# Attention, output projection and gated MLP on one core: when a unit's loads and the chain of its outputs are issued

## Chip, core and metric

The kernel runs on one core of a Trainium2 chip. The metric is the device time of one execution in microseconds (us), lower is better. Before the change the median of 3 runs is 2955.37 us (2953.96 to 2956.3).

## The reference, cut

```python
def _A_ref(x, wqkv, wo):                       # B = 1, S = 2048, D = 576
    H = 32; Dh = D // H                        # 32 heads of 18
    qkv = (x @ wqkv).reshape(B, S, 3, H, Dh).transpose(2, 0, 3, 1, 4)
    q, k, v = qkv[0], qkv[1], qkv[2]
    p = _softmax(einsum("bhqd,bhkd->bhqk", q, k) * Dh ** -0.5, axis=-1)
    o = einsum("bhqk,bhkd->bhqd", p, v)
    return o.transpose(0, 2, 1, 3).reshape(B, S, D) @ wo
def _B_ref(x, w_gate, w_up, w_down):           # F = 4608
    return (sigmoid(x @ w_gate) * (x @ w_up)) @ w_down
...
h = _layernorm(x) * (1 + ca) + sa
x = x + ga * _A_ref(h, A_wqkv, A_wo)
h = _layernorm(x) * (1 + cb) + sb
return x + gb * _B_ref(h, B_w_gate, B_w_up, B_w_down)
```

All is float32; the six vectors sa, ca, ga, sb, cb, gb come from a small product of a condition vector with `w_mod`.

## The kernel before

The program has three stages: layer norm and projections of q, k and v (to about 229 us of the trace), attention (229 to 1604 us), and the MLP (to the end). The change is in attention.

**Units and steps.** Attention is cut into 32 units, `u` = 0 to 31. A unit is a pair of heads on one half (1024) of the queries: units 0 to 15 take the first half, 16 to 31 the second. A unit has 16 steps (`kt` = 0 to 15 in the code; this text counts them 1 to 16), one for each block of 128 keys. In a step TensorE makes four score tiles (L916) of 128 keys x 512 queries, ScalarE takes their exponentials (L920), and `values()` (L539) multiplies the exponentials of two steps back by the values and by a column of ones, so that the sums of the softmax come out as a row of the output.

**Maxima.** The softmax needs the maximum of each query, and it is made by a second set of score tiles, in `maxima()`: 64 tiles to a unit, four in each step, made 22 steps ahead of the unit that uses them. So the maxima of unit u+1 end in step 10 of unit u, and those of u+2 begin in step 11. VectorE reduces each tile (L452). In most units ("paired" ones) one tile of eight goes to ScalarE instead (L455, a copy through Relu) and is joined to another by VectorE (L457). In units 0, 1, 16 to 18 and 27 to 29 (`SINGLE`) all are reduced alone. After the 64th tile VectorE runs a short chain, here called **the maxima's end**: reduce (L464), transpose (L466), cast (L468), subtract (L469). Then the maxima go through DRAM into rows of the queries' tile (L470, L475).

Score tiles of both kinds rotate through seven banks of PSUM (`bank()`): a tile's matmul waits until the bank's tile of seven tiles ago has been read.

**Loads of heads.** `load_heads(u + 2)` (L413 to L421) issues eight transfers on SyncE's queue (SP), some 1.5 MB, into the tiles that unit u-1 has freed. It stands at the end of step 2.

**Outputs.** The 512 queries x 4 result of unit u-1 is complete in step 1 of unit u. In step 2 ScalarE copies it out (L553), and `outputs()` gives a list of things to do; every even step takes one off the list (the letter `w` in the order of a step). Before the change the list is `[gather, spread, None, None, scaled, None, stored]`, so:

- step 2, `gather`: a transfer (SP, L571) brings the sums into a 128x16 tile;
- step 4, `spread`: VectorE's reciprocal (L574), a transfer of it to DRAM (SP, L575), and a transfer that reads it back over 128 partitions (SP, L576);
- step 10, `scaled`: GpSimd multiplies, casts and subtracts (POOL, L579 to L581);
- step 14, `stored`: four transfers to `od` in DRAM (SP, L592).

**Work beside it.** At the letter `w` also stands one turn of `rows0` (from step `FROM0`, unit 15) or of `rows1` (from step `FROM1`, unit 27). `rows0` first prepares the weights of the output projection on GpSimd (`load_wo`), then idles eight turns, then projects the first half (`project_o(0, 8)`, matmuls L676, loads of `od` L645 and L650 and of x L652 on SP, each tile of 128 rows in two turns and loaded a tile ahead), then runs layer norm and makes operands for the MLP (L767, L716 to L727, GpSimd). `rows1` projects most of the second half (`project_o(8, 16)`).

**What sets the order.** In attention TensorE, VectorE and SP run in the order in which the code is written. ScalarE and GpSimd are put in order by the scheduler when the program is built. Every engine runs its own instructions strictly in its order, and each instruction of SP's waits, with all behind it, for what it needs.

## Time and profile before

| | |
|---|---|
| median of 3 runs | 2955.37 us |
| the profiled execution's own time | 2952.37 us |
| its span in the trace | 2950.6 us |
| busy: TensorE (PE), VectorE (DVE), ScalarE (ACT), GpSimd (POOL) | 97%, 75%, 53%, 23% |
| granted TensorE clock, mean | 0.987 |
| an ordinary paired unit | 39.5 to 40.2 us |
| units 17 and 18, 28 and 29 (with projection) | 53.4 and 54.7, 54.3 and 54.3 us |

A row of a timeline gives start, duration, engine, line, operation, `out<-in`, shapes, how many in a row, and in brackets the idle time of the engine before it with what ended it. A row of a table of windows gives a stretch `from:to`, its length, and for each engine the busy time with the count of instructions, then the granted clock (1.00 is full speed), the busy share of the DMA engines, and GB/s. `SPq` is SyncE's queue, where a row's duration is that of issuing a transfer, not of the transfer itself.

### The profile page before, as it was taken

To read this page: it belongs to the slowest core of one execution; us is meant where nothing else is said; L and a number is where in the kernel's file an instruction comes from. 1 tells how busy PE (TensorE), PEld (TensorE's weight loads), DVE (VectorE), ACT (ScalarE), POOL (GpSimd) and SP (SyncE) were. 2 spreads that over 40 slices of the span, in tenths; PEclk is the share of its full clock that TensorE was granted. 3 is DMA by queue.
4 is the path that set the end of the run, shared out by engine and by line. 5 is a ranking of instruction groups with operands and counts; after the bars stand their busy time and mean duration, and the time that the engine had idled before them with its cause. 6 is when DMAs were issued, how large, how long until landed. Compare 5 with 4: busy or idle time off the path is not lost.

```text
span 2950.6 us, 46231 instructions
## 1 busy us (share of the span) xinstructions
PE 2848.5 (97%) x16901; PEld 1876.0 (64%) x16901; DVE 2215.6 (75%) x4047; ACT 1570.4 (53%) x2908; POOL 684.8 (23%) x793
## 2 busy tenths in 40 slices
PE   7999999999999999999999899988999999999999
PEld 6863333333344534334443788877888888888888
DVE  7278889999999789999872778878877555555555
ACT  3217889999977688898678323333333111111111
POOL 3112025455221007730103322233222100000000
PEclk9999999999999999999999999999999999999999
DMA  5343244444223312321344776677555845545443
GB/s 178 123 160 87 65 125 156 155 144 135 88 79 92 109 54 92 111 74 59 101 132 153 273 239 228 234 256 249 207 200 211 321 159 176 170 167 167 165 157 136
DMA packets 177135, 456.26 MB, mean 155 GB/s; under 512 B 36488, under 2 KB 86412, under 8 KB 164620
## 3 DMA queue, kind: packets, MB, share of 16 engines
q1 hardware_dynamic: 162140, 376.72, 38.8%
q0 software_dynamic: 14768, 76.59, 7.4%
q8 instruction: 133, 2.18, 0.3%
q14 instruction: 94, 0.77, 0.1%
HBM read 285.07 MB, written 167.91 MB: 154 GB/s over the span
## 4 chain that ended last, share of the span: by engine, by line
PE 77%; DVE 11%; DMA 4%; issue 3%; ACT 3%; SPq 1%; POOL 1%; POOLq 0%; DVEq 0%; ACTq 0%
PE o L539 15%; PE d L1055 14%; PE x L1019 12%; PE s L446 10%; PE s L916 10%; PE bg L1019 4%; PE bu L1019 4%; DVE mx L452 4%; PE s L276 4%; PE s L327 2%; ACT p L920 2%; PE s L676 2%; DVE w L1011 1%; DMA xs<-ho 1%; DMA t<-od 1%
## 5 line engine op out<-in xcount | busy, mean ns | idle before, releaser
L452 DVE TENSOR_REDUCE mx<-s 128x1 f32<-128x512 f32 x1664 | 1057.3, 684 | 130.8 <-PE s L446 109.5
L920 ACT ACTIVATE p<-s 128x512 f32<-128x512 f32 x2048 | 1064.3, 611 | 165.6 <-PE s L916 80.8
L446 PE MATMUL s<-k,q 54*128 54x512 f32 x1920 | 610.4, 451 | 14.7 <-ACT p L920 6.3
L916 PE MATMUL s<-q,k 56*128 56x512 f32 x1920 | 559.0, 429 | 11.6 <-DVE mx L452 8.0
L539 PE MATMUL o<-p,vaug 128*32 128x512 f32 x4096 | 560.4, 612 | 0.4 <-ACT p L920 0.4
L1055 PE MATMUL d<-wd,hh 128*128 128x288 f32 x2304 | 475.5, 301 | 27.9 <-DVE Oa L1059 25.7
L446 PEld LDWEIGHTS s<-k,q 54*128 54x128 f32 x1920 | 278.2, 186 | 281.7 <-ACT p L920 225.1
L916 PEld LDWEIGHTS s<-q,k 56*128 56x128 f32 x1920 | 263.5, 187 | 300.1 <-DVE mx L452 216.1
L1055 PEld LDWEIGHTS d<-wd,hh 128*128 128x128 f32 x2304 | 378.4, 191 | 44.0 <-DVE Oa L1059 33.6
L1059 DVE TENSOR_TENSOR Oa<-Oa,d 128x288 f32<-128x288 f32 x576 | 256.0, 452 | 133.3 <-PE d L1055 129.0
L1055 PE MATMUL d<-wd,hl 128*128 128x288 f32 x1152 | 343.8, 298 | 0.0
L1019 PE MATMUL x<-k,w 128*128 128x512 f32 x1008 | 244.3, 393 | 4.2 <-ACT w L1010 4.2
L1055 PEld LDWEIGHTS d<-wd,hl 128*128 128x128 f32 x1152 | 220.1, 191 | 0.0
L1019 PEld LDWEIGHTS x<-k,w 128*128 128x128 f32 x1008 | 188.8, 190 | 43.8 <-ACT w L1010 5.6
L1031 ACT ACTIVATE u<-u 128x512 f32<-128x512 f32 x72 | 45.4, 631 | 320.2 <-DVE u L1207 316.2
L539 PEld LDWEIGHTS o<-p,vaug 128*32 128x32 f32 x4096 | 84.0, 108 | 167.7 <-issue 155.8
L1028 ACT ACTIVATE sg<-x 128x512 f32<-128x512 f32 x36 | 21.6, 599 | 315.7 <-PE x L1019 315.6
L1061 POOL DMA_DIRECT2D out_dram<-Oa x16 | 8.7, 544 | 604.3 <-DVE Oa L1059 604.3
L455 ACT ACTIVATE over<-s 128x512 f32<-128x512 f32 x192 | 114.6, 597 | 37.9 <-PE s L446 32.3
L457 DVE CUSTOM_DVE_ANT_0 over<-s,over 128x512 f32<-128x512 f32 x192 | 129.4, 674 | 0.0
L1019 PE MATMUL x<-big,w 128*128 128x512 f32 x504 | 120.5, 390 | 2.2 <-issue 2.2
L1019 PE MATMUL x<-w,w 128*128 128x512 f32 x504 | 121.2, 390 | 0.0
(211 smaller groups left out, 3555.0 us busy)
## 6 DMA issues: line engine op xcount, KB each, us to landing
ws<-w SPq DMA_DIRECT2D x126, 640.0 KB
w<-ws SPq DMA_DIRECT2D x126, 640.0 KB
wd<-wds SPq DMA_DIRECT2D x36, 1152.0 KB
k<-kd SPq DMA_DIRECT2D x60, 360.0 KB
wds<-w POOLq DMA_DIRECT2D x18, 1152.0 KB, 5.5
k<-kd SPq DMA_DIRECT2D x60, 180.0 KB
w<-in_B_w_down_dram POOLq DMA_DIRECT2D x18, 576.0 KB, 5.1
q<-qd SPq DMA_DIRECT2D x64, 144.0 KB
```

The lines of the kernel that those rows point to most:

```text
L276: nc.tensor.matmul(acc, w, hT[:, t, cols], start=n == 0, stop=n == len(ts_) - 1)
L327: nc.tensor.matmul(acc[:, 0:HALF], hT[:, k, rows], w, start=n == 0, stop=n == len(ts_) - 1,)
L446: nc.tensor.matmul(sp, qs[rows, qt * P : (qt + 1) * P], ks[rows, at * 512 : (at + 1) * 512], start=True, stop=True,)
L452: nc.vector.tensor_reduce(to, sp, axis=AX.X, op=ALU.max)
L455: nc.scalar.activation(over, sp, AF.Relu)
L457: nc.vector.tensor_tensor_reduce(out=over, in0=sp, in1=over, scale=1.0, scalar=LOWEST, op0=ALU.add, op1=ALU.max, accum_out=mx[:, h * n + q ...
L539: nc.tensor.matmul(acc[32 * j : 32 * j + 32, :], vaug[:, kt, (2 * p + h) * VW : (2 * p + h) * VW + 32], probs[2 * c + h], start=kt == 0, s ...
L916: nc.tensor.matmul(sT, ks[rows, kcols], qs[rows, c * 512 : (c + 1) * 512], start=True, stop=True)
L920: state["exp"] = nc.scalar.activation(pr, sT, AF.Exp, scale=SCALE)
L1019: nc.tensor.matmul(acc[v], w[:, v, a, :], X[s][:, b, :], start=first and n == 0, stop=n == 6, skip_group_check=not first,)
L1055: nc.tensor.matmul(acc[:, :HALF], a[:, f, rows], w[:, f, cols], start=n == 0, stop=n == 5)
L1059: nc.vector.tensor_add(Oa[:, t, cols], Oa[:, t, cols], acc[:, :HALF])
```

## The change

`load_heads(u + 2)` moves from the end of step 2 to the start of the unit. `spread` is split: the reciprocal and its transfer to DRAM become `inverted`, the read back remains `spread`, and the list becomes `[gather, None, None, inverted, spread, None, scaled, stored]`, that is steps 2, 8, 10, 14 and 16. Since outputs are stored one turn later, `load_wo` idles nine turns and `FROM1` is two steps later: both projections, and all that follows in `rows0`, move by two steps.

```diff
-FROM0, FROM1 = 15 * 16, 27 * 16 + 13
+FROM0, FROM1 = 15 * 16, 27 * 16 + 15
...
-        def spread():
+        def inverted():
             nc.vector.reciprocal(rec, sums)
             nc.sync.dma_start(rows_r.rearrange("j (q e) -> (j q) e", e=16), rec)
+
+        def spread():
             nc.sync.dma_start(full, rows_r.unsqueeze(1).to_broadcast([4, 32, 512]))
...
-        return [gather, spread, None, None, scaled, None, stored]
+        return [gather, None, None, inverted, spread, None, scaled, stored]
...
         weights.extend((wo_h, wo_l, we))
-        for _ in range(8):
+        for _ in range(9):
             yield
...
         qs, ks = heads(u)
+        if 0 < u < UNITS - 2:
+            load_heads(u + 2)
...
             pending.append((half, p, kt, probs))
-            if 0 < u < UNITS - 2 and kt == 1:
-                load_heads(u + 2)
```

Lines below the split stand two to four further down after it: `spread` is L578, the stores L594, the loads of `od` L647 and L652, of x L654, the scores L920, the exponentials L924.

On SP, at the turn from unit 16 to unit 17, where the first projection starts, there stood these rows (stores of unit 15's outputs, five loads for the first projected tile, the gather, the next tile's first load):

```order
L592 DMA od<-big 18x2x512 x4
L645 DMA t_11968<-od 128x4x128
L650 DMA t_11968<-od 64x128
L645 DMA t_11968<-od 128x4x128
L650 DMA t_11968<-od 64x128
L652 DMA Oa<-in_A_x_dram 128x576
L571 DMA sums<-oT 128x1x16
L645 DMA t_12043<-od 128x4x128
```

and now stand these:

```order
L594 DMA od<-big 18x2x512 x4
L413 DMA q_984<-qd 36x1x1024
L416 DMA q_984<-qd 18x1024
L417 DMA k_2193<-kd 36x1x2560
L421 DMA k_2193<-kd 18x2560
L413 DMA q_984<-qd 36x1x1024
L416 DMA q_984<-qd 18x1024
L417 DMA k_2193<-kd 36x1x2560
L421 DMA k_2193<-kd 18x2560
L571 DMA sums<-oT 128x1x16
L647 DMA t_12045<-od 128x4x128
L652 DMA t_12045<-od 64x128
```

The first tile's loads have moved from ahead of the eight loads of heads to behind them. On SP in unit 28, in the second projection, the piece behind the loads of heads was (reciprocal out, read back, then a projected tile's loads):

```order
L421 DMA k_2190<-kd 18x2560
L575 DMA rows_r<-rec 128x16
L576 DMA big<-rows_r 128x1x512
L645 DMA t_18809<-od 128x3x128 x2
L652 DMA raw_18812<-in_A_x_dram 128x576
```

and is now:

```order
L421 DMA k_2190<-kd 18x2560
L571 DMA sums<-oT 128x1x16
L647 DMA t_18713<-od 128x3x128 x2
L654 DMA raw_18716<-in_A_x_dram 128x576
L647 DMA t_18870<-od 128x3x128 x2
L654 DMA raw_18873<-in_A_x_dram 128x576
L575 DMA rows_r<-rec 128x16
L578 DMA big<-rows_r 128x1x512
```

Two tiles' loads now stand ahead of the reciprocal's transfer and the read back, none between or just behind them. On ScalarE, in step 9 of unit 9 (numbers on the names are kept; `s0` to `s6` are the banks, `over` is the tile that goes through Relu), there stood:

```order
L920 ACTIVATE p2_7691<-s5_7689 128x512
L455 ACTIVATE over_7702<-s0_7700 128x512
L920 ACTIVATE p1_7706<-s1_7704 128x512
L920 ACTIVATE p0_7710<-s2_7708 128x512
L920 ACTIVATE p3_7720<-s5_7718 128x512
```

and now:

```order
L924 ACTIVATE p2_7690<-s5_7688 128x512
L924 ACTIVATE p1_7705<-s1_7703 128x512
L924 ACTIVATE p0_7709<-s2_7707 128x512
L455 ACTIVATE over_7701<-s0_7699 128x512
L924 ACTIVATE p3_7719<-s5_7717 128x512
```

The Relu, which frees bank s0, has moved behind two exponentials. The scheduler does so in step 9 of 21 units: 1 to 14 and 19 to 25, by one place in units 1, 19 and 23 and by two in the others.

## The prediction

> **What bounds the kernel now.** I read the chain of work that ended last, then what SP's queue waited for, then step by step the windows of attention, and timelines at the steps that stand out.

> ```profile
> PE 77%; DVE 11%; DMA 4%; issue 3%; ACT 3%; SPq 1%; POOL 1%; POOLq 0%; DVEq 0%; ACTq 0%
> SPq L576 <- DMA rows_r<-rec: 232.0, 32, 14.5
> ```

> TensorE carries the chain. SP stands 232.0 us in 32 waits (7.3 us each) at the read back (L576) until the reciprocals have landed in DRAM. That is no loss by itself: what counts is what stands behind it in the queue. The next rows are SP's in unit 28, and TensorE's first matmul of the projected tile loaded there.

> ```profile
> 1435.90 0.36 SPq L575 DMA_DIRECT2D rows_r<-rec  x1
> 1442.78 0.60 SPq L576 DMA_DIRECT2D big<-rows_r  x1
> 1443.47 1.02 SPq L645 DMA_DIRECT2D t<-od  x2
> 1450.88 0.58 PE L676 MATMUL s<-w,t 128*128 128x288 f32 x1 [4.35 <-DMA t<-od]
> ```

> The read back held SP until 1442.78, the tile's loads went out behind it, and TensorE then idled 4.35 us for them. The windows show what such places cost; in each the counted instructions are TensorE's score matmuls (L916). The first seven are steps 11 and 12 of units 0, 13, 24, 16, 22, 23, 27; the last four are steps 6 and 8 of unit 28, and of unit 29.

> ```profile
> 260.42:265.53 5.11, 2.77 (x8) 1.36 (x8) 1.00 0.05 10
> 789.76:794.91 5.15, 2.26 (x8) 1.09 (x8) 1.00 0.06 12
> 1285.11:1290.55 5.44, 2.37 (x8) 1.23 (x8) 1.00 0.04 8
> 915.88:923.72 7.84, 3.60 (x8) 1.67 (x8) 0.78 0.04 8
> 1199.79:1206.46 6.67, 2.37 (x8) 1.23 (x8) 1.00 0.32 115
> 1241.95:1250.59 8.64, 2.44 (x8) 1.37 (x8) 0.84 0.17 51
> 1407.36:1415.21 7.85, 3.57 (x8) 1.62 (x8) 0.78 0.03 6
> 1440.03:1443.65 3.62, 1.15 (x5) 0.37 (x3) 1.00 0.15 35
> 1445.89:1456.21 10.32, 1.44 (x5) 0.47 (x3) 0.67 0.61 146
> 1494.90:1498.80 3.90, 1.43 (x5) 0.55 (x3) 1.00 0.23 51
> 1501.04:1510.93 9.89, 1.71 (x5) 0.65 (x3) 0.65 0.61 162
> ```

> Steps 11 and 12 take 5.11 and 5.15 us undisturbed, but 7.84 and 7.85 in units 16 and 27, 6.67 and 8.64 in 22 and 23. Step 8 takes 10.32 us in unit 28 where step 6 takes 3.62. The granted clock is below 1.00 in most of these. The steps around 11 suffer from GpSimd, as unit 16 shows:

> ```profile
> 916.93 1.19 DVE L468 CAST parts<-turned 128x32 fp32r<-128x32 f32 x1
> 918.16 0.65 DVE L469 TENSOR_TENSOR parts<-turned,parts 128x32 fp32r<-128x32 f32 x1
> 916.80 1.28 POOL L579 TENSOR_TENSOR big<-big,oT 128x512 f32<-128x512 f32 x1
> 918.15 0.61 POOL L580 CAST big<-big 128x512 fp32r<-128x512 f32 x1
> ```

> The cast and subtract of the maxima's end, 0.18 and 0.19 us in unit 14 below, last until GpSimd's multiply and cast of the outputs are over. I call that a collision.

> **The change, part by part**, against the profiled execution (2952.37 us, 3.0 under the median shown).

> (a) *The read back no longer stands ahead of a projected tile's loads.* In units 28 and 29 those loads now go out ahead of the reciprocal. Gone: (10.32 - 3.62) + (9.89 - 3.90) = **-12.7 us**. What is late next there is (b).

> (b) *Heads' loads ahead of a projected tile's loads.* How long they fill the queue is seen in unit 14:

> ```profile
> 808.14 0.80 SPq L413 DMA_DIRECT2D q<-qd  x1
> 813.61 0.36 SPq L575 DMA_DIRECT2D rows_r<-rec  x1
> 821.23 0.59 SPq L576 DMA_DIRECT2D Oa<-rows_r  x1
> 1543.70 0.34 SPq L575 DMA_DIRECT2D rows_r<-rec  x1
> 1545.13 0.57 SPq L576 DMA_DIRECT2D big<-rows_r  x1
> ```

> A small transfer issued right behind the loads has landed 821.23 - 808.14 = 13.1 us after the first of them went out; in unit 30, without such loads (last two rows), it takes 1.43 us. [...] Now unit 17, before:

> ```profile
> 933.85 0.50 PE L916 MATMUL s<-q,k 56*128 56x512 f32 x1
> 936.65 1.85 PE L676 MATMUL s<-w,t 128*128 128x288 f32 x12
> ```

> A projection's matmuls begin 2.80 us into the unit in step 2. After the change the first tile's are in step 4, two steps (5.11 us) later, at 7.9 us. Its loads stand behind the loads of heads, which cannot begin before the unit does. They land not before 13.1 us; by themselves they take up to 7.4 us (1443.47 to 1450.88, with the read back ahead). I take 15.7, nearer to the first, since part of the transfer passes beside the heads'. TensorE idles 7.8 us. In unit 28 an idle time of 4.35 cost 6.70, so 2.35 are added for the lower clock behind it: **+10.1 us** (0 if the loads pass the others, 14.9 if the 7.4 follow the 13.1). The same in step 6 of units 28 and 29, where the tile is needed at 14.5 and 15.0 us: 1.2 + 0.7 = **+1.9 us** (0 to 6).

> (c) *When GpSimd multiplies.* The scaling is written in step 14, but GpSimd isn't tied to steps: it starts when the read back lands. In unit 14 (first row: its start):

> ```profile
> 804.64 0.40 PE L916 MATMUL s<-q,k 56*128 56x512 f32 x2
> 812.08 1.29 DVE L452 TENSOR_REDUCE mx<-s 128x1 f32<-128x512 f32 x2 [0.27 <-PE s L446]
> 813.29 0.24 DVE L574 RECIPROCAL rec<-sums 128x16 f32<-128x16 f32 x1
> 821.82 1.29 DVE L452 TENSOR_REDUCE mx<-s 128x1 f32<-128x512 f32 x2 [0.29 <-PE s L916]
> 829.73 0.18 DVE L468 CAST parts<-turned 128x32 fp32r<-128x32 f32 x1
> 829.94 0.19 DVE L469 TENSOR_TENSOR parts<-turned,parts 128x32 fp32r<-128x32 f32 x1
> 826.11 1.29 POOL L579 TENSOR_TENSOR Oa<-Oa,oT 128x512 f32<-128x512 f32 x1 [36.23 <-DMA Oa<-rows_r]
> ```

> Before, the multiply began at 826.11, 4.88 us behind the read back's issue, and GpSimd was done at about 829.4, just ahead of the cast. Now the reciprocal stands four steps later, behind the reduces that begin at 821.82 as it stood behind those of 812.08, 1.21 us from their start: at 823.03. The transfer goes out 0.32 later (813.61 - 813.29), the read back 1.43 after that, the multiply 4.88 after that: 823.03 + 0.32 + 1.43 + 4.88 = **829.66**, against a cast at 829.73 and a subtract at 829.94. It is a tie, and each of the two must be over, or GpSimd's multiply (1.28 us) holds it. Only a multiply later than 830.1 misses both. So where GpSimd is otherwise idle the collision that units 16 and 27 had stays, and units 2, 14, 24, 25, 26 get it. In units 4 to 13 other work stands ahead of the multiply on GpSimd, and nothing moves. The price of one: 1.53 (6.67 - 5.14) to 3.5 (8.64 - 5.14), 2.7 in units 16 and 27. I take 2.0, as some will hit only the subtract: 5 x 2.0, less the 0.3 that unit 24 has already (5.44): **+9.7 us**. Ends: 5 x 3.5 = 17.5, and -5.7 if units 16 and 27 too are spared. In units 20 to 23 GpSimd is busy with the layer norm's work, two steps later than before; 5.0 us of collisions stand there now (1.5 and 3.5), which may shrink or double; I take 0.

> [...]

> ```profile
> 916.70:920.10 3.40, 2.13 (x15) 0.57 (x13) 3.33 (x6) 2.01 (x5) 3.25 (x4) 1.00 0.07 14
> 920.10:923.50 3.40, 3.40 (x15) 1.28 (x15) 3.40 (x6) 2.12 (x4) 0.00 (x1) 0.50 0.02 4
> ```

> 1.27 us of idle time in 3.40 were enough for a clock of 0.50 in the next 3.40. [...]

> (d) *Relu two exponentials later in step 9.* The order on ScalarE changes in 21 units. Unit 9, before:

> ```profile
> 626.62 0.60 ACT L455 ACTIVATE over<-s 128x512 f32<-128x512 f32 x1
> 627.11 2.27 ACT L920 ACTIVATE p<-s 128x512 f32<-128x512 f32 x4
> 628.20 0.50 PE L446 MATMUL s<-k,q 54*128 54x512 f32 x1
> ```

> The matmul at 628.20 needs the Relu's bank. With two exponentials ahead, about 0.5 us each, the Relu ends at 628.2 to 628.6 instead of 627.22: 0 to 0.45 us late. I take 0.15, as short delays are taken up elsewhere: 21 x 0.15 = **+3.2 us** (0 to 9).

> (e) *At nothing:* the reciprocal is one 0.24 us instruction in either place. The loads themselves are needed in step 11, 24 us into a unit, and land 13 us into it now, 16 before. SP at the read back no longer waits behind loads; nothing else waited for that.

> Sum: -12.7 + 10.1 + 1.9 + 9.7 + 3.2 = **+12.2 us**, so 2964.6 against the profiled execution and 2967.6 against the median; I say **2966**.

> **Rivals.** *The collisions miss* (for it: the tie is 0.1 to 0.4 us from it, and read backs may take longer; against: the Relu's delay moves the cast towards the multiply). From a multiply 0.5 us later on, (c) is -5.7: sum -3.2, 2952. *The projected tile isn't held* (for it: the loads of heads may not use all of the queue; against: the 13.1 us). If it lands within 7.9 us of unit 17's start, (b) is 0: sum +0.2, 2955. *Both*, the other side: -15.2, 2940; that is the change with its stall removed and nothing in its place, faster as soon as the multiply is 0.5 us late and the tile not held. *The wait moves to the reciprocal:* the gather now stands behind the loads of heads, and if the sums land after the 18.4 us at which VectorE comes to the reciprocal (823.03 in the unit that starts at 804.64), VectorE stands still in some 28 units, 28 us for each us late. Against it: by (b) they land by 13.5. With this, or with collisions at 3.5 and a late Relu, 2975 to 2990.

> **How the numbers follow.** Forecast 0.48; collisions miss 0.17; tile not held 0.10; both 0.15; worse 0.10. A measurement of this kernel can tell 0.2% from no change, here 5.9 us, 2949.5 to 2961.3. Faster: both, and a part of the missed collisions, 0.20. Same: the rest of these two rivals and the forecast's lower edge, 0.25. Slower: 0.55. The range leaves out the worst and the far end of "both": 2938 to 2982.

> **What would show it.** Right: in units 28 and 29 no step 8 near 10 us; in unit 17 TensorE idle 5 us or more ahead of L676 in step 4, ended by the load of `od`; cast or subtract over 1 us in units 2, 14, 24 to 26; SP's waits at the read back near 1.4 us each. Wrong: steps 11 and 12 at 5.1 in those units and in 16 and 27, a reciprocal that waits for the gather, or step 9 or 10 longer by more than 0.5 us.

## The result, and the profile after

The changed kernel takes **2980.51 us** (median of 4 runs, 2979.04 to 2984.88) against 2954.66 (4 runs, 2951.38 to 2956.3): **1.0092** times as long, 95% interval 1.0076 to 1.0107, some 26 us slower. The profiled execution has a span of 2977.3 us against 2950.6, and a mean granted clock of 0.985 against 0.987. Attention took 28.7 us more; what lies before and after it, 2.0 less.

In the rows below the multiply is L581 and the projection's matmul L678.

SP's wait at the read back, 232.0 us before, is down to 65.5 us, 2.2 us each where the prediction expected near 1.4:

```profile
SPq L578 <- DMA rows_r<-rec: 65.5, 30, 6.3
```

The windows of the changed kernel, counted instructions TensorE's score matmuls. In order: step 8 of units 28 and 29; step 4 of unit 17; steps 11 and 12 of units 22 and 14; step 16 of unit 30.

```profile
1478.28:1481.89 3.61, 1.12 (x5) 0.37 (x3) 1.00 0.03 2
1527.10:1530.98 3.88, 1.39 (x5) 0.55 (x3) 1.00 0.05 8
952.07:964.81 12.74, 1.28 (x5) 0.47 (x3) 0.73 0.83 157
1223.80:1240.18 16.38, 3.07 (x8) 1.53 (x8) 0.69 0.26 97
841.33:849.40 8.07, 2.54 (x9) 1.44 (x8) 0.87 0.08 17
1591.09:1600.54 9.45, 0.96 (x6) 0.51 (x6) 0.88 0.54 181
```

And step 4 of unit 17 in the kernel before:

```profile
942.60:946.88 4.28, 1.12 (x6) 0.38 (x4) 1.00 0.61 183
```

The two stalls of step 8 (10.32 and 9.89 us) are gone. In their place stand unit 17 (12.74 us, 4.28 before), unit 22 (16.38 us in two steps, 6.67 before), unit 14 (8.07, 5.74 before) and, at a place the prediction didn't name, step 16 of unit 30 (9.45 us, 2.23 before). Steps 11 and 12 of unit 15 fell from 9.09 us to 5.82, and those of unit 24 (5.14) weren't hit.

Three places follow, one at a time. First **unit 17**, which starts at 944.72:

```profile
942.61 0.81 SPq L413 DMA_DIRECT2D q<-qd  x1
948.84 0.49 SPq L647 DMA_DIRECT2D t<-od  x1
958.99 3.35 PE L678 MATMUL s<-w,t 128*128 128x288 f32 x11 [6.29 <-DMA t<-od]
```

The loads of heads go out from 942.61 on, 2.1 us before the unit's first score matmul. The first projected tile's loads are issued from 948.84 on, behind them, and the tile has landed 14.3 us into the unit (958.99 - 944.72), 16.4 us after the first load of heads went out. TensorE idles 6.29 us.

Then **unit 22**, VectorE ahead of GpSimd and TensorE:

```profile
1224.33 6.67 DVE L468 CAST parts<-turned 128x32 fp32r<-128x32 f32 x1
1231.04 3.52 DVE L469 TENSOR_TENSOR parts<-turned,parts 128x32 fp32r<-128x32 f32 x1
1226.71 1.27 POOL L729 TENSOR_TENSOR t<-t 128x512 f32<-128x512 f32 x1
1227.93 1.27 POOL L581 TENSOR_TENSOR big<-big,oT 128x512 f32<-128x512 f32 x1
1229.15 1.26 POOL L729 TENSOR_TENSOR t<-t 128x512 f32<-128x512 f32 x1
1230.36 0.60 POOL L582 CAST big<-big 128x512 fp32r<-128x512 f32 x1
1230.91 0.60 POOL L718 CAST ho<-t 128x512 fp32r<-128x512 f32 x1
1235.21 0.79 PE L920 MATMUL s<-q,k 56*128 56x512 f32 x1 [9.54 <-DVE mx L452]
```

A cast of 0.18 us lasts 6.67 and the subtract behind it 3.52, while GpSimd runs one operation of the layer norm or of the outputs after another without a pause, the issue of a transfer (L721, 0.79 us from 1225.89) among them. TensorE idles 9.54 us.

Last **unit 30**: the changed kernel, and then the kernel before at the same place.

```profile
1577.67 0.56 SPq L578 DMA_DIRECT2D big<-rows_r  x1
1578.32 0.43 SPq L853 DMA_DIRECT2D raw<-in_B_w_gate_dram  x1
1582.43 4.82 SPq L470 DMA_DIRECT2D rows_m<-parts  x1
1595.86 3.25 SPq L475 DMA_DIRECT2D q<-rows_m  x4
1600.54 1.19 PE L920 MATMUL s<-q,k 56*128 56x512 f32 x3 [7.15 <-DMA q<-rows_m]
```

```profile
1545.79 0.43 SPq L851 DMA_DIRECT2D raw<-in_B_w_gate_dram  x1
1560.36 0.34 SPq L470 DMA_DIRECT2D rows_m<-parts  x1
1564.90 1.43 SPq L475 DMA_DIRECT2D q<-rows_m  x2
```

Behind the read back, SP's queue holds loads of the MLP's second block of weights (`raw`; the first block goes by GpSimd's queue, paced to step 8). Before, SP's went out 11 us into the unit, 15 us ahead of the maxima's rows (L470), and those had landed 4.5 us after their issue (1564.90 - 1560.36). Now they go out at 21 us, together with GpSimd's, and the rows take 13.4 us. Unit 31's first score matmul waits for them.

### The profile page after: what moved, and what is told of

Its sections match the earlier page's. It is cut to its first block, busy times and chain, and to the rows that moved or that the text cites. A ratio compares the mean times of both kernels' runs of the same rounds, so it can differ in the third digit from the quotient of the medians.

```text
span 2977.3 us, 46248 instructions
## 1 busy us (share of the span) xinstructions
PE 2856.9 (96%) x16901; PEld 1880.2 (63%) x16901; DVE 2231.9 (75%) x4047; ACT 1570.3 (53%) x2908; POOL 685.4 (23%) x793
## 3 DMA queue, kind: packets, MB, share of 16 engines
q1 hardware_dynamic: 162140, 376.72, 38.8%
## 4 chain that ended last, share of the span: by engine, by line
PE 76%; DVE 12%; DMA 5%; issue 3%; ACT 3%; SPq 1%; POOL 0%; POOLq 0%; DVEq 0%; ACTq 0%
PE o L539 15%; PE d L1057 13%; PE x L1021 11%; PE s L446 10%; PE s L920 10%; DVE mx L452 4%; PE bg L1021 4%; PE bu L1021 4%; PE s L276 4%; PE s L327 2%; ACT p L924 2%; PE s L678 2%; DVE w L1013 1%; DMA xs<-ho 1%; DVE parts L468 1%
## 5 line engine op out<-in xcount | busy, mean ns | idle before, releaser
L924 ACT ACTIVATE p<-s 128x512 f32<-128x512 f32 x2048 | 1065.4, 611 | 190.7 <-PE s L446 99.6
L452 DVE TENSOR_REDUCE mx<-s 128x1 f32<-128x512 f32 x1664 | 1057.2, 684 | 137.3 <-PE s L446 116.0
L446 PE MATMUL s<-k,q 54*128 54x512 f32 x1920 | 609.4, 452 | 13.8 <-ACT p L924 5.9
L920 PE MATMUL s<-q,k 56*128 56x512 f32 x1920 | 565.7, 431 | 33.1 <-DVE mx L452 23.8
L920 PEld LDWEIGHTS s<-q,k 56*128 56x128 f32 x1920 | 266.6, 188 | 323.4 <-DVE mx L452 234.3
L446 PEld LDWEIGHTS s<-k,q 54*128 54x128 f32 x1920 | 277.2, 186 | 282.9 <-ACT p L924 221.7
L1021 PEld LDWEIGHTS x<-k,w 128*128 128x128 f32 x1008 | 187.1, 188 | 42.1 <-ACT w L1012 4.3
L455 ACT ACTIVATE over<-s 128x512 f32<-128x512 f32 x192 | 114.7, 598 | 41.2 <-PE s L446 37.5
```

The lines of the kernel that those rows point to most:

```text
L446: nc.tensor.matmul(sp, qs[rows, qt * P : (qt + 1) * P], ks[rows, at * 512 : (at + 1) * 512], start=True, stop=True,)
L452: nc.vector.tensor_reduce(to, sp, axis=AX.X, op=ALU.max)
L455: nc.scalar.activation(over, sp, AF.Relu)
L920: nc.tensor.matmul(sT, ks[rows, kcols], qs[rows, c * 512 : (c + 1) * 512], start=True, stop=True)
L924: state["exp"] = nc.scalar.activation(pr, sT, AF.Exp, scale=SCALE)
L1021: nc.tensor.matmul(acc[v], w[:, v, a, :], X[s][:, b, :], start=first and n == 0, stop=n == 6, skip_group_check=not first,)
```

## The experiments

All times are medians; the kernel before, measured beside them, had medians of 2953.4 to 2954.1 us. Step numbers and profiles are those of each kernel's profiled execution. That is one execution, and the collisions are not the same in each. The changed kernel and, of the experiments below, e3, e4 and e5 have the same instructions in the same order on each of VectorE, ScalarE, GpSimd and SP up to unit 15, yet unit 1 takes 46.9, 46.9, 49.2 and 53.4 us in their traces, unit 10 44.0, 40.2, 40.8 and 40.2, and unit 14 43.4, 40.8, 44.8 and 42.1. So a difference of some us in the collisions of one unit can be chance.

### e1: only the loads moved

```diff
 (the kernel before)
+        if 0 < u < UNITS - 2:
+            load_heads(u + 2)
...
-            if 0 < u < UNITS - 2 and kt == 1:
-                load_heads(u + 2)
```

> The kernel before with one thing of the change: heads' loads first in the unit (the list of the outputs' chain, the 8 idle turns and FROM1 as before). Theory A (the loss of the change comes from the chain's later places, from unit 17's first tile behind the heads' loads and from the ninth idle turn; heads' loads first by itself is harmless): here the first projected tile is fetched in step 16 of unit 16, ahead of unit 17's loads, so unit 17 stays near 53 us; the read back goes out 13 us into a unit instead of 16.6, so GpSimd multiplies some 3.5 us earlier, at 18 us, and the collisions of units 15, 16 and 27 (before: steps 11 to 13 of unit 15 some 4.9 us too long, units 16 and 27 some 2.7 each) go; in units 28 and 29 the tile's loads go out 3.5 us earlier and step 8 falls from 10 to 4 to 6 us. Sum -15 to -20 us against the kernel before: about 2937. Rival B (heads' loads first are the costly part, since the gather and the reciprocal wait behind them): VectorE would wait in the 4th step's reciprocal of some 28 units, 2970 or more.

Measured: **3069.76 us**, ratio 1.0398 (1.0379 to 1.0417). Theory A fell here, and rival B held, far above the 2970 that it named as its least. VectorE's reciprocal of e1 as a group (busy, mean ns, idle time ahead; 22.3 in the kernel before); then the window of step 5 of unit 9:

```profile
L574 DVE RECIPROCAL rec<-sums 128x16 f32<-128x16 f32 x32 | 8.1, 252 | 108.1 <-DMA sums<-oT 108.1
```

```profile
667.75:673.98 6.23, 1.50 (x5) 0.68 (x4) 0.91 0.51 198
```

The sums stand behind 1.5 MB of loads, and the reciprocal in step 4 waits for them: 86 us more idle time of VectorE ahead of it, 3.72 of them in unit 9, where step 5 takes 6.23 us instead of 2.14. Steps 5 and 6 account for 131 us more over all units. So with the loads first the reciprocal can't stay in step 4: its later place isn't a side of the change that could be left out. Step 8 of units 28 and 29 is 3.60 and 3.89 here too.

### e2: only the new places and the ninth turn

```diff
 (the changed kernel)
-        if 0 < u < UNITS - 2:
-            load_heads(u + 2)
...
+            if 0 < u < UNITS - 2 and kt == 1:
+                load_heads(u + 2)
```

> The changed kernel with heads' loads back at the end of step 2; the new list, the nine idle turns and FROM1 kept. Theory A: unit 17's first tile is fetched in step 2 ahead of the heads' loads, so its step 4 is near 4.3 instead of 12.7 us (-8.5); unit 22's step 11 stays at 12 us, since it comes from the ninth turn; in units 28 and 29 the tile's loads still stand behind the heads' loads, which now go out 6 us later, so of the 12.7 us saved in step 8 some 0 to 8 come back. Sum -8.5 to 0 against the changed kernel: about 2975. Rival B (heads' loads first are the costly part): most of the 26 us goes, 2955 to 2960. Step 10 longer by 0.24 us in the units with Relu stays by A, since the list made it.

Measured: **2973.37 us**, 1.0062 (1.005 to 1.0075). The windows of step 2 of unit 16, and of steps 11 and 12 of unit 22; then ScalarE's timeline in unit 16:

```profile
898.48:906.82 8.34, 1.43 (x6) 0.47 (x4) 0.67 0.22 80
1213.98:1227.09 13.11, 3.08 (x8) 1.69 (x8) 0.68 0.34 125
```

```profile
902.61 0.58 ACT L553 COPY oT<-o 128x512 f32<-128x512 f32 x1 [4.25 <-POOL Oa L581]
```

As expected, unit 17's 8.5 us are gone (step 4 takes 4.26) and unit 22's collision stays. New are 5.5 us in unit 16: in this build GpSimd's multiply stood behind the preparation of the projection's weights, and ScalarE's copy of the next outputs waited 4.25 us for it. In units 28 and 29 nothing of the stall of step 8 came back (3.61 and 3.89 us). The profiled execution (2964.44 us) is the fastest of the five and 9 us under their median, so the steps do not add up to the measured difference. The expectation on step 10 was wrong: it is back at 2.74 us, so it isn't the list alone that lengthens it. In the trace of e1 and e2 the Relu of unit 9 runs ahead of the exponentials of step 9, as before; in the changed kernel and in e3, where step 10 takes 2.97 or 2.98, it stands behind two of them.

### e3: eight idle turns

```diff
 (the changed kernel)
-        for _ in range(9):
+        for _ in range(8):
```

> The changed kernel with 8 idle turns instead of 9 ahead of the first rows' projection (the first tile is then fetched in step 16 of unit 16, right behind the stores of the outputs). Theory A (the projection's and the layer norm's work stand one pair of steps later against the units because of the ninth turn, and that puts GpSimd's unbroken row of operations on the maxima's end of unit 22): unit 17 step 4 back to 4.3 us (-8.5), unit 22 step 11 back to 2.1 to 3.5 us (-8.5 to -10), unit 20 down by 3 us: about 2959. Rival C (the collision of unit 22 comes from the scaling, which the new list sets 22 us into the unit): step 11 of unit 22 stays near 12 us, and only unit 17's 8.5 us go: about 2972.

Measured: **2957.15 us**, 1.0012 (1.0002 to 1.0022): 23 of the 26 us are gone. The windows of step 4 of unit 17, steps 11 and 12 of unit 22, step 16 of unit 30:

```profile
947.44:951.71 4.27, 1.13 (x5) 0.37 (x3) 1.00 1.03 161
1205.12:1212.93 7.81, 2.67 (x10) 1.48 (x8) 0.80 0.42 155
1566.62:1575.34 8.72, 0.95 (x5) 0.51 (x6) 0.78 0.57 187
```

With eight turns the first tile is loaded in step 16 of unit 16, ahead of unit 17's loads, and the layer norm's operations run two steps earlier against the maxima's end. Rival C falls: the list was as in the changed kernel, and the cast in unit 22 lasts 1.12 us instead of 6.67. Unit 30 is nearly as it was. Of what steps 11 to 13 give back in this trace, units 10 and 14 have 3.7 and 2.9 us, ahead of the place where the edit begins to act; by the traces above that part is chance.

### e4: the loads second in unit 17 alone

```diff
 (the changed kernel)
-        if 0 < u < UNITS - 2:
+        if 0 < u < UNITS - 2 and u != 17:
             load_heads(u + 2)
...
+            if u == 17 and kt == 1:
+                load_heads(u + 2)
```

> The changed kernel, but in unit 17 alone heads' loads stay at the end of step 2, behind the loads of the first projected tile. If the tile is late because heads' loads stand ahead of it: step 4 of unit 17 falls from 12.7 to 4.3 us and nothing else moves, -8.5: about 2972. If the tile is late for another reason (its 16 features' stores in the step before, the stores of outputs on the same queue): step 4 stays near 12.7, about 2980.

Measured: **2973.26 us**, 1.006 (1.0048 to 1.0073). The number is as expected, the way to it isn't. The window of step 8 of unit 17, and from the timeline what TensorE waits for there:

```profile
965.08:974.39 9.31, 1.12 (x5) 0.38 (x3) 0.82 0.62 165
```

```profile
968.68 0.50 PE L678 MATMUL s<-w,t 128*128 128x288 f32 x2 [2.97 <-DMA t<-od]
```

Step 4 lost its 8.48 us (4.26), but step 8 gained 5.06: now the second tile stands behind the loads of heads. Unit 17 is 3.9 us shorter; the other 3.5 of attention's gain are for the most part collisions in other units (10, 16, 20 and 23 shorter; 1, 14, 22 and 27 longer), which the edit doesn't aim at.

### e5: unit 30's chain in its old places

```diff
 (the kernel of e3)
+        if half and p == 13:
+            return [gather, lambda: (inverted(), spread()), None, None, scaled, None, stored]
         return [gather, None, None, inverted, spread, None, scaled, stored]
```

> The kernel of e3 (the changed kernel with 8 idle turns; there step 16 of unit 30 takes 8.72 us against 2.23 before, and unit 31 34.2 against 32.5), but the outputs of unit 29, whose chain runs in unit 30, have the places of before (reciprocal and read back in step 4, scaling in step 10, stores in step 14). Theory A: SP's four loads of the feed-forward's block stand behind the read back in SP's queue; read back in step 8 instead of 4, they go out beside GpSimd's block loads and hold the maxima's rows for unit 31. With the old places they go out 10 us earlier: step 16 of unit 30 back to 2.2 to 3 us, unit 31 back to 32.5, -7 to -8.5 us: about 2949. Rival D (GpSimd's paced block loads alone hold the rows): step 16 stays near 8.7, 2957.

Measured: **2955.47 us**, 1.0003 (0.9992 to 1.0013), a miss in the sum. The windows of steps 5 and 16 of unit 30, and the reciprocal in the timeline:

```profile
1546.53:1553.00 6.47, 1.79 (x6) 0.79 (x4) 0.73 0.25 74
1576.31:1578.54 2.23, 0.96 (x5) 0.48 (x6) 1.00 0.49 123
```

```profile
1548.35 0.25 DVE L574 RECIPROCAL rec<-sums 128x16 f32<-128x16 f32 x1 [3.04 <-DMA sums<-oT]
```

Step 16 fell to 2.23 us, so SP's block loads were what held the maxima's rows. GpSimd's alone don't: they begin 20.1 us into the unit in the changed kernel and in the kernel before, where step 16 takes 2.23 us. Rival D falls. But step 5 rose by 4.33 and step 6 by 1.16: in this kernel the projection ends two steps later, GpSimd's loads of the MLP's operands run beside the gather, and the reciprocal in step 4 waits 3.04 us for the sums.

### e6: the new places in units 28 and 29 alone

```diff
 (the kernel before, with spread split as in the change)
+        if half and p in (11, 12):
+            return [gather, None, None, inverted, spread, None, scaled, stored]
+        return [gather, lambda: (inverted(), spread()), None, None, scaled, None, stored]
```

> The kernel before, with the new places (reciprocal step 8, read back step 10, scaling step 14, stores step 16) for the outputs of units 27 and 28 alone, whose chain runs in units 28 and 29. Heads' loads, idle turns and FROM1 as before. Theory A: step 8 of units 28 and 29 falls from 10.3 and 9.9 to 3.6 and 3.9 us, since the read back no longer stands ahead of the tile's loads; nothing else changes: -12.7, less up to 2 us for a multiply nearer to the maxima's end there: about 2943. Rival B (the stall in step 8 goes only because heads' loads are first): step 8 stays at 7 us or more, 2950 to 2955.

Measured: **2939.57 us**, 0.9955 (0.9943 to 0.9967). Step 8 of units 28 and 29:

```profile
1447.92:1451.53 3.61, 1.13 (x5) 0.37 (x4) 1.00 0.13 35
1496.77:1500.65 3.88, 1.40 (x6) 0.56 (x4) 1.00 0.06 11
```

Attention is 12.3 us shorter; these two steps give 12.73, and collisions elsewhere come and go by up to 2.4 us (unit 12 longer, unit 15 shorter), in units that run the same order as before. Rival B falls. The part of the change that pays is a read back that no longer stands ahead of a projected tile, in two units.

### e7: the turned maxima in PSUM

```diff
 (the changed kernel)
-            turned = small.tile([P, 32], F32, name="turned", bufs=1)
+            turned = bank()[:, 0:32]
```

> The changed kernel with one edit in the maxima's end: the turned maxima are put in a PSUM bank instead of SBUF, so that VectorE's cast (L468) reads PSUM only and its subtract (L469) has one operand in SBUF. Theory A (the cast and the subtract wait for GpSimd because both engines read SBUF there): cast and subtract take about 0.2 us each in every unit, whatever GpSimd does; step 11 of unit 22 falls from 12.0 to about 2.5, and units 10, 13, 14, 16, 20, 22, 23, 26 to 29 lose their long steps 11 to 13: -25 to -33 us against the changed kernel, 2948 to 2956. Rival E (what they wait for is something else, the writes to the parts tile or VectorE's own queue): the collisions stay, 2978 to 2985.

Measured: **2947.26 us**, 0.9981 (0.9973 to 0.999), 33 us under the changed kernel and below the kernel before. Cast and subtract in groups, first in the changed kernel, then in e7; then e7's timeline in unit 22, VectorE's cast ahead of the GpSimd operation that runs beside it:

```profile
L468 DVE CAST parts<-turned 128x32 fp32r<-128x32 f32 x32 | 20.5, 639 | 1.1
L469 DVE TENSOR_TENSOR parts<-turned,parts 128x32 fp32r<-128x32 f32 x32 | 19.2, 599 | 1.1
```

```profile
L468 DVE CAST parts<-s 128x32 fp32r<-128x32 f32 x32 | 6.1, 191 | 1.1
L469 DVE TENSOR_TENSOR parts<-s,parts 128x32 fp32r<-128x32 f32 x32 | 6.1, 191 | 1.1
```

```profile
1207.67 0.19 DVE L468 CAST parts<-s 128x32 fp32r<-128x32 f32 x1
1207.44 1.27 POOL L720 TENSOR_TENSOR t<-t,t 128x512 fp32r<-128x512 f32 x1
```

Both last 0.18 to 0.19 us in each unit whatever GpSimd does; rival E falls. Steps 11 to 13 are 38.8 us shorter than in the changed kernel (21.0 above the kernel before, now 17.8 below it, since it had collisions too); step 10 is some 0.2 us longer in most paired units, 6 us in all, which gives a part back. The chance goes too: units 1 to 15 take the same time to 0.06 us in the traces of e7, e9 and e10.

### e8: e6 and PSUM

The edits of e6 and e7 together, on the kernel before.

> The kernel of e6 (before, with the new places for units 28 and 29 alone) with the turned maxima in a PSUM bank as in e7. Theory A: the two gains add: -12.7 for step 8 of units 28 and 29, and the collisions that the kernel before has in units 15 (4.9 us), 16 and 27 (2.7 each), 22 and 23 (1.5 and 3.5), some 15 us: about 2927. If PSUM costs the score matmuls a bank at the wrong time: 2940 or more. If the collisions aren't about SBUF (rival E): as e6, 2943.

Measured: **2932.58 us**, 0.9932 (0.9919 to 0.9946): 7 us under e6 instead of 15. The collisions of units 15, 16, 22, 23 and 27 are gone, but step 10 is 0.4 us longer in some 20 units, and step 2 of unit 16 takes 6.98 us instead of the 3.03 of e6; ScalarE's copy waits 3.03 us there for GpSimd's multiply, as in e2. Why step 10 pays for a tile more in the rotation of the banks was not tried.

### e9 and e10: PSUM with eight turns, and unit 30

```diff
 (the changed kernel, with the edits of e3 and e7; e10 in addition)
+        if half and p == 13:
+            return [gather, None, inverted, spread, None, scaled, stored]
         return [gather, None, None, inverted, spread, None, scaled, stored]
```

> The changed kernel with the turned maxima in PSUM (as in e7, 2947 us) and 8 idle turns (as in e3). If the collisions and the order of loads are separate costs: only what the ninth turn costs without collisions is gained over e7, step 4 of unit 17 (8.5 us, less the 1.4 that step 2 regains) and the projection's last half in unit 19 (1.3): -8 us, about 2939. If e3's gain came from the collisions alone, nothing is gained: 2947.

Measured: **2940.20 us**, 0.995 (0.9934 to 0.9965), 7 us under e7: step 4 of unit 17 is 4.25 us, unit 19 1.2 us shorter. The order of loads and the collisions are separate costs.

> The kernel of e9 with the outputs of unit 29 (chain in unit 30) at steps 2 gather, 6 reciprocal, 8 read back, 12 scaling, 14 stores. In e5, with the reciprocal in step 4, the loss moved from step 16 to step 5, since the sums landed 11.7 us into the unit and VectorE waited 3.04 us for them. Step 6 comes at 13.5 us, behind that landing. If that reading holds: step 5 stays at 2.1 and step 7 at 2.1, and step 16 falls from 8.7 to about 2.2 to 4 with unit 31 at 32.5: -6 to -8 us against e9, about 2932. If SP's block loads, 3 us later than in e5, still hold the maxima's rows: step 16 near 6 to 9, 2937 to 2939.

Measured: **2929.10 us**, 0.9915 (0.9898 to 0.9931), the fastest here. The window of step 16 of unit 30 (step 5 takes 2.12 us):

```profile
1550.77:1552.99 2.22, 0.95 (x5) 0.48 (x5) 1.00 0.16 57
```

With the reciprocal in step 6 the sums have landed, and SP's loads are out early enough: 6.6 us in unit 30 and 1.1 in unit 31 gone. With e5 and the kernel before, that settles the cause of unit 30. The median fell by 11 us, more than the 6 to 8 expected; of the rest the traces show 1.5 us in unit 20 and some 2 us before and after attention, which this edit doesn't explain.

## Why the prediction was right in sign and short in size

The sign was right and the time lies in the range, 1.5 us under its upper end; the sum was less than half of what came. That the range held is in part luck, as (c) and the rivals below show. By attention's steps, changed kernel less kernel before, in us:

| term | forecast | measured |
|---|---|---|
| (a) step 8, units 28 and 29 | -12.7 | -12.7 |
| (b) step 4, unit 17 | +10.1 | +8.5 |
| (b) step 6, units 28 and 29 | +1.9 | 0.0 |
| (c) collisions, steps 11 to 13 of all units, one execution of each | +9.7 | +21.0 |
| (d) Relu, step 10 | +3.2 | +3.0 |
| unit 30 step 16 to unit 31 step 2 | not named | +8.4 |
| rest of attention | 0 | +0.6 |
| sum | +12.2 | +28.7 |

**(a)** held to a tenth of a microsecond. e6 shows that the new places alone do it, e1 that the earlier loads alone do it as well.

**(b)** The mechanism was right: the tile landed at 14.3 us instead of 15.7, and TensorE idled 6.29 us instead of 7.8. But two errors met here. The loads of heads "cannot begin before the unit does", says the prediction; they began 2.1 us before, and the tile took 16.4 us from there instead of 15.7. Step 4 grew by 2.2 us more than the idle time, at a clock of 0.73; 2.35 were forecast for a lower clock. Step 2, which no longer projects, is 1.4 us shorter, which was left out. In units 28 and 29 the tile of step 6 came in time (3.61 and 3.89 us, as before). There the loads of heads began 2.1 and 3.0 us before the unit, and a tile has two transfers fewer, since L652 is not issued for the second half; which of the two made it timely was not separated.

**(c)** is the step that failed, in where and how much. The time worked out for unit 14 was right; here are the reciprocal, its transfer, the read back, the multiply and the cast, and then the subtract and the multiply of unit 24:

```profile
834.94 0.24 DVE L574 RECIPROCAL rec<-sums 128x16 f32<-128x16 f32 x1
835.21 0.35 SPq L575 DMA_DIRECT2D rows_r<-rec  x1
836.65 0.58 SPq L578 DMA_DIRECT2D Oa<-rows_r  x1
841.62 1.28 POOL L581 TENSOR_TENSOR Oa<-Oa,oT 128x512 f32<-128x512 f32 x1 [37.71 <-DMA Oa<-rows_r]
841.86 1.09 DVE L468 CAST parts<-turned 128x32 fp32r<-128x32 f32 x1
```

```profile
1319.65 0.19 DVE L469 TENSOR_TENSOR parts<-turned,parts 128x32 fp32r<-128x32 f32 x1
1320.20 1.27 POOL L581 TENSOR_TENSOR big<-big,oT 128x512 f32<-128x512 f32 x1 [7.14 <-DMA big<-rows_r]
```

The multiply starts 25.1 us into unit 14 (841.62, the unit at 816.56), as worked out (829.66 - 804.64 = 25.0), just ahead of the cast, and the unit pays 2.9 us. But the 1.43 us from the transfer to the read back, taken from unit 30, are 2.2 to 2.7 in units 2, 24 and 25; there the multiply starts behind the subtract, and nothing is hit. Unit 26 is hit in the subtract alone (1.16 us, +0.95). So of the five named units two were hit. That unit 14 is one of them is luck: with the same order, in the trace of e3, the multiply begins 0.1 us behind the start of the subtract (838.98), and neither is held:

```profile
838.76 0.18 DVE L468 CAST parts<-turned 128x32 fp32r<-128x32 f32 x1
839.08 1.28 POOL L581 TENSOR_TENSOR Oa<-Oa,oT 128x512 f32<-128x512 f32 x1 [38.30 <-DMA Oa<-rows_r]
```

The tie that was worked out falls to either side from one execution to the next. Against that stand units named as unmoved or taken at nothing:

- **Unit 22, +9.7 us.** "I take 0" for units 20 to 23 was the single largest error. The layer norm's operations stood two steps later because of the ninth turn: the cast of unit 22 lasts 6.67, 6.13 and 6.68 us in the three traces with nine turns (changed kernel, e2, e4) and 1.12 and 1.15 in e3 and e5. And the price of a collision was bounded by 3.5 us, when in a row of GpSimd operations without a pause the cast alone was held for 6.67.
- **Unit 20, +4.3, and unit 13, +1.5**, by the same kind of collision. Unit 20's cast lasts 1.33 to 1.35 us with nine turns and under 0.5 in e3 and e5. In unit 13 the multiply was taken to stand behind other work.
- **Unit 10, +4.2 us**: "nothing moves" in units 4 to 13. This one is not shown to belong to the change. The later Relu of (d) puts the maxima's end 0.26 us later into the unit (24.83 instead of 24.57), but in e3 and e5 it stands there too (24.81 and 24.82), and unit 10 takes 40.2 us instead of 44.0.
- **Unit 15, -4.6, and unit 27, -1.3**: collisions of before that went. Unit 15's was one with the preparation of the projection's weights; why that moved out of the way was not followed. In e6, which keeps the old order there, it is 2.4 us smaller too.

So the step that failed is the price and the place of (c): 9.7 us for five named units, where two of them cost 3.9, units 20 and 22, taken at nothing, cost 14.0, and the rest goes up and down with the execution. That these steps are long by collisions is shown by e7, in which no cast or subtract lasts over 0.19 us and steps 11 to 13 are 38.8 us shorter with one tile moved.

**(d)** was right in place, and its sum by two errors against each other: 0.21 to 0.25 us in step 10 of 16 units, where 0.15 in 21 were taken, and 0.4 us less in units 17 and 20 each.

**Unit 30** was missed because the read back was followed only to what attention has behind it. Behind the last read backs SP's queue holds the MLP's first loads; under (e) the prediction has "nothing else waited for that". Its own rule, that what counts is what stands behind a wait in the queue, was not applied there.

Of the rivals, *the wait moves to the reciprocal* did not come in the changed kernel, where the only reciprocal with idle time ahead is the last, behind attention; e1 shows it with the reciprocal left in step 4, at 115 us. The time came out inside the range that the prediction gave its worst case (2975 to 2990), but not by what it named there: the reciprocals didn't wait, and it wasn't five collisions of 3.5 us, but units 17, 20, 22 and 30.

On the collision's cause: before and after the change the reduce L464 lasts 0.21 to 0.22 us and the transpose L466 0.21 in all 32 units, also in unit 22 of the changed kernel (1223.83 and 1224.09), where GpSimd runs beside them. The cast behind them takes up to 1.37 us before the change and 6.67 after it, the subtract up to 1.30 and 3.52. With the turned maxima in PSUM, the cast's only operand and one of the subtract's two, both take 191 ns in the mean. The cast was held through several GpSimd instructions in a row (6.67 us in unit 22). By what means GpSimd holds it was not shown.

What stays open: why the read back goes out 1.4 us behind the transfer in some units and 2.2 to 4.5 in others, when a held cast gets its turn, why step 10 pays for e7's extra tile, and what decides whether the clock drops after a short idle time (below).

## What to carry to other kernels

A step that is moved in a queue carries along whatever the scheduler hung behind it: follow the queue to the next stage's first loads, not to the end of the loop. When a wait is moved, ask of each thing that then goes first who stood behind it: e1, e4 and e5 each removed a wait and found one again at another consumer. A tie between two engines is not to be forecast by a tenth of a microsecond, since it falls otherwise in the next execution of the same order (unit 14's cast took 1.09 us in one trace and 0.18 in another); it is to be removed. The turned maxima in PSUM were worth 33 us on the changed kernel and 7 on e6, where the reordering itself had gained 14.

## What the runs showed of the hardware

- A cast of 0.18 us was held 6.67 us in unit 22, until 1231.00, through GpSimd operations that follow each other without idle time. In unit 14, where GpSimd leaves 0.07 us between its multiply (to 842.90) and its cast (from 842.97), VectorE's cast ended in that pause, after 1.09 us. So the price of a collision was not bounded by one operation. Nor was it the whole row: the cast of unit 22 ended about where one GpSimd cast gave way to the next (1230.91), while the row went on until the subtract's end and beyond.
- After a short idle time the clock did not follow its length. In the changed kernel TensorE's longest idle time was 1.26 us in step 11 of unit 13, and 0.95 us in unit 10. The windows are steps 11 and 12 of unit 13, and 11 to 13 of unit 10; the longer one left the clock at 1.00, the shorter one was followed by 0.50 for 6.83 us, a mean of 0.70:

```profile
800.16:806.82 6.66, 2.37 (x8) 1.23 (x8) 1.00 0.04 10
675.39:686.95 11.56, 4.44 (x14) 2.26 (x12) 0.70 0.39 139
```
